# Chunk-selected attention and a phase mixer: query loads of the first groups, an engine for each cast and triangle, token weights by TensorE

## The chip, the cores and the metric

The kernel runs on one core of a Trainium2 chip. The metric is the device time of one execution in microseconds (us). Engines are called PE (TensorE; PEld is its weight load), DVE (VectorE), ACT (ScalarE), POOL (GpSimd) and SP (SyncE, which here only issues DMA transfers). Each engine takes its own instructions strictly in order. Sixteen DMA engines carry the transfers that SP issues.

## The reference

Batch 4, 8 heads, 768 tokens, head size 64; then a mixer over the 512 channels that the heads make together.

```python
k_min, k_max = min and max of k over chunks of 32 tokens          # 24 chunks
ub  = sum_d maximum(q * k_min, q * k_max)                         # per query and chunk
ub  = where(query's chunk >= chunk, ub, -1e9);  top = 6 largest chunks
s   = where(chunk selected and key <= query, q @ k.T / 8, -1e9)
x   = softmax(s) @ v                                              # heads side by side: 768 x 512
theta = x @ w_theta;  zr, zi = x * cos(theta), x * sin(theta)
u   = x + w_tok_r @ zr + w_tok_i @ zi                             # over tokens, 768 x 768 each
out = u + maximum(u @ w_ch, 0)
```

## The kernel before, in words

The work is cut into small tasks. Each is registered by `plan.add` (L36) with the engine that runs it, a duration, what it reads and writes, and a function that emits its instructions. If the engine is given as a table of two, either may run it. The numbers in the table `ORDER` (L153) say in which order all tasks are emitted; a negative entry stands for the task whose number is its complement, on the second engine of its table. `emit` (L62) goes through this list, and so the list alone fixes the order on every engine and in SP's queue. The durations take no part in that.

A *group* (b, g) is half a batch: four heads. For each group:

- `load_kc` (L264) loads the keys of four heads (768 KB, for the first group in two halves), `load_q` (L277) the queries of a pair of heads, 192 KB a head, into a tile `q32` of 128 partitions x 6 blocks x 2 heads x 64, and `load_v` (L286) the values, 96 KB a time. The query view `(n p) d -> p n d` puts token 128n + p on partition p: a partition gets six single rows of 256 B.
- `keys` (L297) takes chunk minima and maxima on DVE (L313, L318, L322) from the fp32 keys. It also casts the keys to fp16 (tile `ke`, L356, POOL), transposes them on PE (L364) and puts them into `kext` (L370, ACT or DVE), the left side of the scores.
- `queries` (L377) transposes the fp32 queries on PE (L399, PSUM tile `psq`), copies them into `ubq` (L405, ACT or DVE) and takes their positive part (L411, POOL or DVE). For the two groups of batch 0 (the set `QPE`, in the code `pe`) `qext`, the right side of the scores, is cast from `ubq` (L417). For all other groups the queries are cast to fp16 into `qe` (L386, POOL), and after the choice a DMA transpose turns `qe` into `qext` (L487).
- `choice` (L422) forms the bounds on PE (L440), adds the causal mask (L448), transposes (L454), finds the six largest by DVE's max of eight (L462) and marks the chunks that are not selected (L476). For batch 0 the marks are transposed on PE (L500, `pss`) and copied into `qext` (L505).
- `values` (L510) casts the values to fp16 on POOL (L514).

`attend` (L523) is one head: scores on PE in three segments (L541, PSUM `psc`), exponentials on ACT (L550, tile `pt`), a triangular mask of 0 and 1 multiplied onto the two diagonal blocks of each segment (`tri`, L561, POOL: 128 x 256 fp16 in place), the product with the values on PE (L575), and the division on DVE (L586, L591) into `x16`. So there are 96 triangles.

`transpose16`, `phases` and `mixer` work on a whole batch: x transposed (L608 by DMA or L619 by PE), theta on PE (L639), sines on ACT (L647), products on DVE (L653), then for each of six blocks of tokens twelve matmuls with `wtokT16` (L681, L683), u (L693), its transpose (L699 by DMA, or L705 by PE and L709), the product with `w_ch` (L717), the last addition (L722) and the store (L726). They run while the next batch attends.

`weights` (L814) loads w_theta and w_ch in four blocks each (`square`, L730: load L733, cast on POOL L734), and the two token matrices in six blocks each (`token`, L737: load L741 of 384 KB, cast on POOL L742). A token block must be transposed. Blocks 2 to 5 (the set `WDMA`) go by a DMA transpose (L746), blocks 0 and 1 by six PE transposes (L754, PSUM `pw`) and a copy into `wtokT16` (L758, ACT or DVE).

At the start 24 `fill` and 12 `rest` tasks run matmuls on zeros (L834, L841) that nothing reads.

Of the kernel before, what the change touches and what calls it, by code (L numbers as in the profile page):

```python
# [75 lines left out]
def kernel(  # L76
# [11 lines left out]
    nc = tc.nc  # L88
    B, H, S, D = q.shape
# [24 lines left out]
    for r in range(96):  # L114
# [39 lines left out]
        17, 0, 15, 3, 14, 8, 2, 4, 1, 5, 13, 82, 6, 113, 114, 115, 70, 83, 19, 85, 20, 21, 63, 22, 23, 64, 24,  # L154
        74, 71, 25, 26, 65, 75, 27, 66, 28, 72, 29, 84, 7, 188, 55, 58, 30, 31, 76, 116, 73, 16, 32, 56, 57, 78,
        90, 86, 33, 91, 69, 34, 289, 92, 77, 67, -94, 290, 87, 9, 35, 79, 36, 89, -89, 37, -95, 80, 126, 117, 81,
        127, 190, 128, 97, 129, 96, 143, 189, 132, 98, 99, 130, 10, 192, 102, 18, 111, 103, 11, 100, 104, 38,
        288, 59, 39, 40, 41, 101, 95, 68, 42, 147, 60, 44, 49, 105, 133, 151, 53, 291, 153, 131, 152, 302, 50,
        46, 62, 134, 54, 301, 304, 135, 154, 118, 106, 120, 303, 305, 107, 191, 61, 139, 193, 306, 108, 174, 121,
        148, 136, 175, 292, 244, 51, 119, 43, 109, 110, -156, 407, 137, 52, 247, 45, 409, 144, 138, 47, 150, 307,  # L160
        -141, 245, 408, 248, 194, 176, 250, 251, 321, 141, 180, 177, 181, 308, -146, -143, 258, 178, 112, -147,
        259, 122, -150, 410, 309, 157, 326, 249, 328, 196, 252, 246, 182, 172, 264, 123, -328, 158, 48, 265, 124,
        156, 329, 179, 325, 293, 261, 310, 262, 296, 183, 125, 184, 185, 272, 195, 275, 420, 12, 163, 159, 273,
        313, 260, 186, 200, 444, 187, 295, 263, 317, 160, 161, 421, 278, 406, 164, 445, 276, 294, 279, 253, 322,
        323, 162, 197, 198, 165, 280, 166, 199, 254, 255, 167, 173, 256, -325, 168, 257, 266, 422, 297, 170, 267,
        286, 311, 423, -172, 312, 201, 344, 298, 299, 204, 269, 268, 616, 345, 169, 300, 358, 277, 274, 346, 618,
        347, 342, 270, 359, 271, -331, -315, -425, 619, 411, 281, 348, 446, 283, 425, 315, 374, 282, 617, 413,
        349, 316, -288, 375, 361, 414, 318, 426, -321, 447, 380, 208, 362, 284, 331, 285, -320, 332, 381, 439,
        343, 205, 360, 364, 350, 365, 336, 333, 351, 372, 334, 377, 373, 388, 337, 335, 352, 615, 415, 412, 382,
        363, 378, 338, 212, 353, 366, 354, 355, 202, 418, 394, 356, 629, 339, 357, 630, -204, 389, 427, 395, 367,  # L170
        631, 632, 340, 206, 369, 379, 416, 391, 376, 435, 209, 215, 417, 392, 431, 368, 210, 370, 371, 207, 211,
        383, 385, 390, 384, 402, 396, 393, 403, 653, 440, 655, 386, 460, 656, 387, 397, 462, -442, 648, 620, 399,
        468, 398, 341, 419, 213, 654, 463, 400, 465, 469, 401, -443, 466, 404, 623, -406, 470, 218, 572, 476,
        732, 464, 467, 216, 214, 575, 436, 480, -438, -439, 622, 443, 461, 221, -658, 477, 478, 217, 481, 471,
        473, 484, 482, 624, 479, 488, 485, 483, 492, 486, 219, 489, 490, 487, 496, 224, 220, 491, 493, 500, 494,
        501, 502, 497, 222, 626, 524, 498, 525, 526, 472, 428, 227, 573, 527, 512, 495, 429, 513, 223, 528, 503,
        504, 514, 499, 576, 733, 627, 625, 578, 586, 529, 474, 430, 225, 574, 579, 634, 505, 600, 226, 230, 587,
        530, 228, 601, 515, 592, 580, 577, 621, 233, 516, 593, 506, 517, 229, 589, 507, 475, 606, 581, 590, 518,
        635, -433, -634, -449, 519, 531, 583, 508, 731, 603, 520, 582, 644, -533, 231, 433, 649, 645, 434, 636,
        536, 584, -652, 594, 647, 537, 236, 650, 538, 734, 640, 604, -647, 539, 591, 234, 540, 607, 541, 449,  # L180
        588, 238, 542, 235, 585, 669, 602, 595, 450, 232, 454, 597, 596, 451, 608, 455, 452, 548, 237, 549, 760,
        598, 453, 550, 736, 240, 551, 456, 239, 552, 605, 457, 242, 599, 735, 764, 560, 553, 458, 609, 745, 746,
        637, 459, 561, 610, 562, 638, 614, 563, 564, 611, 243, 565, 554, 241, 639, 670, 612, 509, 566, 641, 671,
        510, 677, 769, 628, 672, 511, 521, 750, 935, 678, 642, 936, 685, 770, 522, 679, 643, 674, 543, 686, 751,
        737, 523, 658, 652, 613, 934, 688, 673, 752, 675, 544, 739, 700, 663, 689, 676, 937, 533, 659, 938, 753,
        701, 703, 680, 740, 681, 555, 704, 690, 534, 682, 771, 742, 714, 754, 556, 738, 772, 705, 683, 545, 715,
        755, 535, 687, 743, 691, 684, 741, 948, 773, 692, 660, 546, 720, 949, 661, 717, 693, 664, 721, 547, -757,
        718, 694, 702, 706, 707, 765, 696, 665, 722, 695, 662, 767, 708, 697, 666, 972, 667, 747, 719, 766, 698,
        709, 953, 711, 973, 748, 710, 974, 699, 567, 557, 757, 568, 716, 712, -976, 713, 728, 758, 761, 558, 723,
        762, 763, 724, 954, 725, 569, 786, 726, -760, 727, 787, 749, 570, 729, 788, 559, 668, 790, 976, -731,  # L190
        950, 955, 785, 774, 791, 939, 951, 956, 793, 801, 943, 794, 792, 775, 944, 891, 779, 802, 789, 776, 945,
        894, 777, 795, 803, 941, 805, 744, 778, 796, 797, 806, 807, 959, 780, 804, 809, 1050, 942, 1051, 781,
        1052, 798, 813, 810, 782, 811, 940, 571, 808, 817, 814, 812, 821, 783, 815, 818, 825, 816, 819, 826, 822,
        827, 820, 823, 892, 824, 957, 828, 847, 848, 958, 836, 837, 829, 830, 849, 850, 799, 1069, 895, 897, 851,
        831, 960, 838, 800, 898, 896, 893, 905, 919, 839, 832, 906, 852, 1070, 961, 908, 840, 841, 920, 853,
        1071, 907, 899, 900, 901, 902, 768, -1076, 962, 909, 967, 947, 1053, 1064, 842, 911, 990, 833, 912, 903,
        843, 991, 904, 933, 834, 835, 858, 922, 910, 923, 859, 1072, -1066, 784, 996, 860, 921, 861, 925, 913,
        952, 997, 862, 993, 914, 863, 926, 963, 864, 994, 988, 916, 915, 1010, 968, 844, 845, 992, 869, 1004,
        969, 924, 854, 971, 970, 1073, 1055, 917, 870, 1066, 1005, 1067, 1068, 927, 871, 964, 872, -967, 1011,
        873, 1054, 874, 918, 965, 995, 875, 1007, 998, 1008, 1074, 928, 930, 929, 1019, 1020, 1058, 946, 865,  # L200
        876, 1006, 977, 931, 1033, 932, 1056, 846, 999, 1001, 1025, 1021, 978, 1057, 982, 1012, 1018, 1000, 1026,
        1076, 855, 1002, 1034, 1009, 1003, 1083, 856, 983, 979, 1013, 980, 857, 1035, 1027, 1014, 1015, 880, 881,
        1022, 1023, 984, 989, 882, 985, 883, 1036, 981, 1079, 1016, 986, 884, 1017, 885, 1024, 1037, 886, 1039,
        1088, 1040, -1090, 1084, 1038, 1028, -1086, 1059, 887, 1041, 1029, 1030, 1077, 1086, 866, 1031, 1032,
        -1079, 1042, 1090, 867, 1062, 1080, -1092, 1043, -1082, 868, 1047, 1044, -1093, 1082, 877, 1106, 1112,
        1045, 878, 987, 1107, 1093, 1046, 1113, 1048, 1094, 1109, 1114, 1049, 888, 1110, 1098, 1095, 1120, 889,
        1111, 1096, 1108, 1210, 1124, 879, 1121, 1097, 1099, 1115, 1213, 1116, 1122, 1100, 1117, 1125, 1128,
        1123, 1126, 1101, 1132, 1129, 1127, 1130, 1136, 1133, 1131, 1134, 1140, 1137, 1135, 1144, 1138, 1145,
        1141, 1139, 1142, 1146, 1147, 1188, 1189, 1143, 1190, 1191, 1148, 1149, 1150, 1192, 1193, 1194, 1118,
        1211, 1214, 1212, 1216, 1217, 1155, 1063, 1177, 1218, 1178, 1224, 1119, 1225, 1179, 1166, 1230, 1215,  # L210
        1102, 1060, 890, 1167, 1061, 1087, 1151, 1103, 1231, 1232, 1219, 1227, 1228, 1168, 1169, 1180, 1156,
        1220, 1226, 1229, 1181, 1238, 1221, 1239, 1240, 1222, 1223, 1241, 1157, 1242, 1182, 1253, 1233, 1183,
        1158, 1159, 1254, 1259, 1160, 1244, 1170, 1235, 1161, 1234, 1260, 1255, 1162, 1261, 1267, 1171, 1199,
# [15 lines left out]

    UDMA = {(b, t) for b in (1, 2) for t in range(NT)} | {(3, t) for t in range(3)}  # L230
    XDMA = {(b, c) for b in (1, 2, 3) for c in range(3)}
    WDMA = {2, 3, 4, 5}

    QPE = {(0, 0), (0, 1)}
    PSUM = {"sc": 2, "av": 1, "mi": 3}
# [662 lines left out]
```

## Time and profile before

| what | value |
|---|---|
| time, median of 6 runs (lowest to highest) | 256.46 us (254.58 to 256.99) |
| the profiled execution: time, and span in the profile | 256.99 us, 255.2 us |
| PE busy, share of the span | 225.8 us, 88% |
| DVE busy | 173.6 us, 68% |
| ACT busy | 164.5 us, 64% |
| POOL busy | 146.5 us, 57% |
| transfers that SP issues, share of 16 engines | 42.63 MB, 74.5% |
| L561 triangles on POOL | 96, 67.2 us, 0.717 each |
| L356 casts of keys on POOL | 16, 19.2 us, 1.197 each |
| L411 positive part: on POOL / on DVE | 8 at 1.789 / 8 at 0.561 us |
| L386 casts of queries on POOL | 12, 10.8 us, 0.903 each |
| L742 casts of token blocks on POOL | 12, 11.3 us, 0.945 each |
| L746 DMA transposes of token blocks | 8, median 4.8 us from issue to landing |
| L754 PE transposes of token blocks / L758 copies | 24, 2.0 us / 3 on ACT at 0.802, 1 on DVE at 0.545 |

"Busy" is the time in which an engine had an instruction in work; what lies between span and time is outside of the instructions. A stage is read by the engine that has no gap in it, a gap by what ended it. In the chain of waits each step is what released the next one, followed back from the last instruction. An engine that is often idle may still be the one that others wait for, since its queue is in order.

### The profile page before, as it was taken

To read this page: it belongs to the slowest core of one execution; us is meant where nothing else is said; L and a number is where in the kernel's file an instruction comes from. 1 tells how busy PE (TensorE), PEld (TensorE's weight loads), DVE (VectorE), ACT (ScalarE), POOL (GpSimd) and SP (SyncE) were. 2 spreads that over 40 slices of the span, in tenths; PEclk is the share of its full clock that TensorE was granted. 3 is DMA by queue.
4 is the path that set the end of the run, shared out by engine and by line. 5 is a ranking of instruction groups with operands and counts; after the bars stand their busy time and mean duration, and the time that the engine had idled before them with its cause. 6 is when DMAs were issued, how large, how long until landed. Compare 5 with 4: busy or idle time off the path is not lost.

```text
span 255.2 us, 5639 instructions
## 1 busy us (share of the span) xinstructions
PE 225.8 (88%) x2124; PEld 142.8 (56%) x2124; DVE 173.6 (68%) x442; ACT 164.5 (64%) x235; POOL 146.5 (57%) x184
## 2 busy tenths in 40 slices
PE   0976878698799996999789999999999999999993
PEld 0545746567564653568655466667555667644441
DVE  2769875997369789799688875878674134742273
ACT  2384799798689770099469877745987685673001
POOL 6474788969784867669594279994304475300000
PEclk9998879999889999799799999999999999999999
DMA  6999899999999999999987828556901926610334
GB/s 175 259 225 240 164 225 268 237 199 274 199 216 210 216 246 232 193 231 208 219 152 192 192 44 181 110 161 136 156 0 30 181 43 140 178 54 0 82 103 164
DMA packets 99394, 42.98 MB, mean 168 GB/s; under 512 B 92568, under 2 KB 92824, under 8 KB 98696
## 3 DMA queue, kind: packets, MB, share of 16 engines
q1 hardware_dynamic: 99368, 42.63, 74.5%
q8 instruction: 16, 0.26, 0.4%
q14 instruction: 10, 0.08, 0.1%
HBM read 26.30 MB, written 6.29 MB: 128 GB/s over the span
## 4 chain that ended last, share of the span: by engine, by line
PE 54%; DMA 14%; ACT 14%; POOL 7%; DVE 4%; issue 3%; SPq 2%; POOLq 0%; ACTq 0%; DVEq 0%
PE psc L541 9%; ACT pt L550 8%; DMA wtokT<-a 7%; PE psy L681 7%; PE psy L683 7%; PE pso L717 6%; PE pst L639 6%; PE psav L575 5%; DMA qext<-qe 4%; POOL pt L561 3%; PE psub L440 2%; PE psq L399 2%; DMA kc<-in_k_dram 2%; ACT kext L370 2%; PE psz L681 2%
## 5 line engine op out<-in xcount | busy, mean ns | idle before, releaser
L550 ACT ACTIVATE pt<-psc 128x1024 f16<-128x1024 f32 (+1 forms) x96 | 84.7, 917 | 29.3 <-PE psc L541 26.3
L561 POOL TENSOR_TENSOR pt<-pt,tri 128x256 f16<-128x256 f16 x96 | 67.2, 717 | 37.5 <-ACT pt L550 37.2
L541 PE MATMUL psc<-qext,kext 88*128 88x512 f16 (+3 forms) x256 | 53.7, 321 | 6.3 <-ACT pt L550 2.7
L681 PE MATMUL psy<-zz,wtokT 128*128 128x512 f16 x120 | 46.2, 385 | 2.4 <-DMA wtokT<-a 2.4
L541 PEld LDWEIGHTS <-kext 88*128 88x128 f16 x256 | 34.7, 152 | 21.6 <-issue 10.3
L683 PE MATMUL psy<-zz,wtokT 128*128 128x512 f16 x120 | 45.9, 383 | 0.0
L575 PEld LDWEIGHTS <-pt 128*128 128x128 f16 x672 | 29.6, 100 | 8.6 <-DVE x L591 2.2
L575 PE MATMUL psav<-v,pt 128*128 128x65 f16 x672 | 32.4, 197 | 1.4 <-DVE x L591 0.7
L313 DVE TENSOR_TENSOR h<-kc 96x1024 f32<-96x1024 f32 (+1 forms) x16 | 21.9, 1366 | 6.5 <-DMA kc<-in_k_dram 6.4
L717 PE MATMUL pso<-wch,uT 128*128 128x512 f16 x96 | 24.6, 384 | 1.5 <-ACT kext L370 1.0
L681 PEld LDWEIGHTS <-wtokT 128*128 128x128 f16 x144 | 14.2, 99 | 16.6 <-DMA wtokT<-a 2.9
L653 DVE TENSOR_TENSOR zz<-x,cs 128x1024 f16<-128x1024 f16 x24 | 17.3, 727 | 9.1 <-ACT cs L647 8.8
L639 PE MATMUL pst<-wtheta,xT 128*128 128x512 f16 x96 | 23.1, 380 | 0.2 <-ACT cs L647 0.2
L722 DVE SCALAR_TENSOR_TENSOR ot<-pso,u 128x512 f32<-128x512 f32 x24 | 16.5, 687 | 9.5 <-PE pso L717 8.8
L693 DVE TENSOR_TENSOR u<-psy,x 128x512 f16<-128x512 f32 x20 | 13.7, 688 | 13.4 <-PE psy L683 13.2
L405 ACT COPY ubq<-psq 128x384 f32<-128x384 f32 (+1 forms) x26 | 10.9, 425 | 17.9 <-PE psq L399 17.7
L683 PEld LDWEIGHTS <-wtokT 128*128 128x128 f16 x144 | 14.2, 99 | 13.9 <-issue 0.9
L356 POOL CAST ke<-kc 96x1024 f16<-96x1024 f32 x16 | 19.2, 1197 | 3.9 <-DMA kc<-in_k_dram 3.9
L647 ACT ACTIVATE cs<-pst,pi 128x512 f16<-128x512 f32 x24 | 16.6, 692 | 7.1 <-PE pst L639 6.7
L399 PE MATMUL psq<-ident,q 128*128 128x128 f32 x84 | 16.8, 315 | 3.9 <-issue 2.3
L370 ACT COPY kext<-pkt 64x768 f16<-64x768 f16 x16 | 12.7, 794 | 11.0 <-PE pkt L364 8.1
L586 DVE RECIPROCAL rec<-psav 128x6 f32<-128x6 f32 x32 | 6.1, 190 | 18.1 <-PE psav L575 17.8
(76 smaller groups left out, 351.8 us busy)
## 6 DMA issues: line engine op xcount, KB each, us to landing
q<-in_q_dram SPq DMA_DIRECT2D x32, 192.0 KB, 4.3
v<-in_v_dram SPq DMA_DIRECT2D x64, 96.0 KB, 3.5
out_dram<-ot SPq DMA_DIRECT2D x24, 256.0 KB, 2.4
kc<-in_k_dram SPq DMA_DIRECT2D x7, 768.0 KB, 7.2
w<-in_moe_w_tok_r_dram SPq DMA_DIRECT2D x6, 384.0 KB, 4.4
w<-in_moe_w_tok_i_dram SPq DMA_DIRECT2D x6, 384.0 KB, 3.9
w<-in_moe_w_theta_dram SPq DMA_DIRECT2D x4, 256.0 KB, 5.6
w<-in_moe_w_ch_dram SPq DMA_DIRECT2D x4, 256.0 KB, 4.8
```

Source lines behind the costliest of these rows:

```text
L313: nc.vector.tensor_tensor(out=st[hn].rearrange("p (z w) d -> p z (w d)", z=2)[:, s], in0=kv[:, s, 0], in1=kv[:, s, 1], op=op)
L356: nc.gpsimd.tensor_copy(out=ke[:, a:a + 16, :], in_=st[kc][:, a:a + 16, :])
L370: (nc.scalar.copy if e == "ACT" else nc.vector.tensor_copy)(out=kext[g][0:D, a + y:a + 16:2, :], in_=st[pkt][y * D:(y + 1) * D])
L399: nc.tensor.transpose(t[:, o * P:(o + 1) * P], st[q32][:, n, :, :].rearrange("p x d -> p (x d)"), ident32)
L541: nc.tensor.matmul(t[:, a0:a1], kx[0:KX, hj:CH * 96:NCH], qx[0:KX, q0 + a0 - o:q0 + a1 - o], start=True, stop=True)
L550: nc.scalar.activation(out=t[:, BASE[s]:BASE[s] + wa + wb], in_=st[psc][:, 0:wa + wb], func=AF.Exp, bias=0.0, scale=scale)
L561: nc.gpsimd.tensor_tensor(out=d, in0=d, in1=tri16.unsqueeze(1).broadcast_to([P, 2, P]), op=ALU.mult)
L575: nc.tensor.matmul(t[:, a, :], st[pt][:, o:o + P], v16s[g][:, x, j, :], start=(j == 0), stop=(j == a))
L639: nc.tensor.matmul(p, st[xT][:, c, t * P:(t + 1) * P], wtheta16[:, c, :], start=(c == 0), stop=(c == 3))
L681: nc.tensor.matmul(acc(), wtokT16[:, i, 0, t * P:(t + 1) * P], st[zz][:, i, 0, :], start=(i == 0), stop=False)
L683: nc.tensor.matmul(acc(), wtokT16[:, i, 1, t * P:(t + 1) * P], st[zz][:, i, 1, :], start=False, stop=(i == NT - 1))
L717: nc.tensor.matmul(p, st[uT][:, c, :], wch16[:, c, :], start=(c == 0), stop=(c == 3))
```

## The change

1. The queries of groups (0,0) and (0,1) are loaded with `(p n) d -> p n d`: partition p gets the tokens 6p to 6p+5, one run of 1536 B in HBM. The tile is the same. PE's transposes then give the columns in another order (block n holds the tokens 6p + n), and the copies L405 of these groups put each column at its place, with a step of six elements on the side they write.
2. The casts of keys, queries, token blocks and square weights, and the triangles, may each go to POOL or DVE.
3. `WDMA` is empty: all twelve token blocks are transposed by PE and copied by ACT or DVE. This makes eight tasks more (1414 for 1406), and all task numbers after them move.
4. `ORDER` is another list throughout. Some of the durations beside the tasks are other numbers, which has no effect of its own.

What the two lists say, counted by engine:

| task | before | after |
|---|---|---|
| triangles (L561) | POOL 96 | POOL 64, DVE 32 (batches 0 to 3: 12, 5, 4, 11 on DVE) |
| casts of keys (L356) | POOL 16 | POOL 13, DVE 3 |
| casts of queries (L386) | POOL 12 | POOL 6, DVE 6 |
| casts of token blocks (L742) | POOL 12 | POOL 8, DVE 4 |
| casts of square weights (L734) | POOL 8 | POOL 7, DVE 1 |
| positive part (L411) | POOL 8, DVE 8 | POOL 2, DVE 14 |
| copies into kext (L370) | ACT 16, DVE 16 | ACT 22, DVE 10 |
| copies of token blocks (L758) | ACT 3, DVE 1 | ACT 9, DVE 3 |
| copies of queries (L405) | ACT 26, DVE 6 | ACT 24, DVE 8 |
| tasks on PE, ACT, DVE, POOL, SP | 522, 227, 279, 178, 200 | 530, 236, 330, 126, 192 |

In SP's queue the eight query loads of batch 0 stand at places 2, 5, 7, 8, 10, 11, 16, 22 before and 2, 5, 6, 8, 9, 11, 12, 14 after; the halves of the first keys at 1 and 6, then 1 and 4; the keys of (0,1) at 9, then 15; the first values at 14, then 18; the causal mask at 12, then 16.

```diff
-    WDMA = {2, 3, 4, 5}
+    WDMA = set()
...
+    def eng(e):
+        return nc.gpsimd if e == "POOL" else nc.vector
...
-                nc.sync.dma_start(out=t[:, :, x, :], in_=q[b, 2 * p + x].rearrange("(n p) d -> p n d", p=P))
+                nc.sync.dma_start(out=t[:, :, x, :], in_=q[b, 2 * p + x].rearrange(
+                    "(p n) d -> p n d" if (b, p // 2) in QPE else "(n p) d -> p n d", p=P))
...
-                nc.gpsimd.tensor_copy(out=ke[:, a:a + 16, :], in_=st[kc][:, a:a + 16, :])
-            plan.add("POOL", 1.1, key, cast, r=rk[0] if a == 0 else rk[-1] if parts == 2 else rk[0], w=[("ke", a)])
+                eng(e).tensor_copy(out=ke[:, a:a + 16, :], in_=st[kc][:, a:a + 16, :])
+            plan.add({"POOL": 1.1, "DVE": 0.68}, None, key, cast, lock=True, r=rk[0] if a == 0 else rk[-1] if parts == 2 else rk[0], w=[("ke", a)])
...
-                nc.gpsimd.tensor_copy(out=qe[:, x0:x0 + 2, :, 0:D], in_=st[q32].rearrange("p n x d -> p x n d"))
+                eng(e).tensor_copy(out=qe[:, x0:x0 + 2, :, 0:D], in_=st[q32].rearrange("p n x d -> p x n d"))
...
-                (nc.scalar.copy if e == "ACT" else nc.vector.tensor_copy)(
-                    out=st[ub][:, QN + t0 + off:QN + t0 + w], in_=st[psq][:, off:w])
+                o, i_ = st[ub][:, QN + t0 + off:QN + t0 + w], st[psq][:, off:w]
+                if pe:
+                    o = st[ub][:, QN:].rearrange("d (p n) -> d n p", n=NT)[:, t0 // P:(t0 + w) // P]
+                    i_ = i_.rearrange("d (n p) -> d n p", p=P)
+                (nc.scalar.copy if e == "ACT" else nc.vector.tensor_copy)(out=o, in_=i_)
...
-                nc.gpsimd.tensor_tensor(out=d, in0=d, in1=tri16.unsqueeze(1).broadcast_to([P, 2, P]),
+                eng(e).tensor_tensor(out=d, in0=d, in1=tri16.unsqueeze(1).broadcast_to([P, 2, P]),
                                         op=ALU.mult)
-            plan.add("POOL", 0.66, key, tri, r=["tri"], w=[(pt, s)])
+            plan.add({"POOL": 0.66, "DVE": 0.28}, None, key, tri, r=["tri"], w=[(pt, s)], lock=True)
...
-        plan.add("POOL", 0.84, key, lambda: nc.gpsimd.tensor_copy(out=new(a), in_=st[n]), r=[n], w=[(a, 0)],
-                 new=[(a, "a16")])
+        plan.add({"POOL": 0.84, "DVE": 0.55}, None, key, lambda e: eng(e).tensor_copy(out=new(a), in_=st[n]), r=[n], w=[(a, 0)],
+                 new=[(a, "a16")], lock=True)
```

The cast of the square weights (L734) is changed in the same way as the last of these.

## The prediction

> **What bounds the kernel now.** I read the busy time in 40 slices first, then stages of it, then the chain of waits where PE (TensorE) stands still. The first view (one digit per 6.4 us, 9 is full):
>
> ```profile
> PE   0976878698799996999789999999999999999993
> ...
> ACT  2384799798689770099469877745987685673001
> ...
> PEclk9998879999889999799799999999999999999999
> DMA  6999899999999999999987828556901926610334
> ```
>
> To see: the 16 DMA engines are full for the first twenty slices (to about 128 us), and from there PE is full to the end. PE's gaps, and the slices in which its clock was granted at 0.7 or 0.8, lie in the part where DMA is full. The same by stage (columns: stretch, length, busy us of PE, PEld, DVE, ACT, POOL with their counts, clock, DMA share, GB/s):
>
> ```profile
> 29.00:59.30 30.30, 25.07 (x334) 19.57 (x334) 25.07 (x80) 27.70 (x39) 24.79 (x33) 0.94 0.93 229
> ...
> 68.20:95.20 27.00, 26.74 (x232) 15.68 (x228) 20.90 (x33) 22.84 (x32) 18.33 (x21) 0.94 1.08 224
> 95.20:108.80 13.60, 11.18 (x95) 6.35 (x85) 11.55 (x36) 0.35 (x3) 9.93 (x14) 0.87 1.10 213
> 108.80:130.70 21.90, 19.35 (x225) 14.45 (x224) 18.01 (x51) 16.56 (x25) 15.39 (x20) 0.92 0.99 216
> 130.70:255.20 124.50, 119.28 (x1014) 69.18 (x1010) 73.75 (x185) 76.44 (x102) 52.69 (x69) 1.00 0.50 113
> ```
>
> From 29 to 59 us ACT is the tightest (27.70 of 30.3) with DVE behind it. From 95 to 109 ACT does 0.35 us of work. From 130.7 on PE is busy 119.3 of 124.5 us, 3.7 of the rest being the end of the span. PE is busy 225.8 of the 255.2 us in all, so 29.4 us are idle: 6.6 before its first instruction, the tail, and some 18 between 7 and 131 us. Only these can be won.
>
> Two places explain most of them. PE around the first scores (start, length, line):
>
> ```profile
> 20.34 0.59 PE L841 MATMUL fill<-zero 128*128 128x122 f16 x8
> 23.23 0.52 PE L399 MATMUL psq<-ident,q 128*128 128x128 f32 x3 [2.30 <-issue]
> ...
> 26.53 0.74 PE L500 MATMUL pss<-ident,a 128*128 128x128 f16 x5
> 28.04 0.59 PE L541 MATMUL psc<-qext,kext 88*128 88x512 f16 x3 [0.77 <-ACT qext L505]
> ```
>
> The choice of group (0,0) leaves DVE at 21.76 us, but its transposes (L500) run at 26.5: PE takes its queue in order, and ahead of them stand the query transposes (L399) of pairs 2 and 3, whose loads were issued between 11.7 and 24 us. And the chain around 95 us:
>
> ```profile
> 88.71 5.06 DMA wtokT<-a
> 93.92 0.83 POOL a L742
> 95.16 1.51 SPq L746
> 96.72 4.87 DMA wtokT<-a
> 101.64 0.39 PE psy L681
> ```
>
> Token weights come through a load, a GpSimd cast and a DMA transpose of about 5 us; mixer(0) waits for the last at 101.6. Query transposes behind it in PE's queue wait too, so ACT stands still.
>
> **The change, part by part.** Prices come from the groups by shape, of which two (count, busy us, mean ns of one, idle before):
>
> ```profile
> L653 DVE TENSOR_TENSOR zz<-x,cs 128x1024 f16<-128x1024 f16 x24 | 17.3, 727 | 9.1 <-ACT cs L647 8.8
> ...
> L619 PE MATMUL psT<-ident,x 128*128 128x128 f16 x42 | 3.8, 232 | 0.0
> ```
>
> (1) *Loads reordered.* In SP's queue the eight query loads of groups (0,0) and (0,1) move from places 2, 5, 7, 8, 10, 11, 16, 22 to 2, 5, 6, 8, 9, 11, 12, 14, past the keys of (0,1) (place 9 to 15) and the first values. The fourteen loads up to the last query hold 2.7 MB (keys 0.79, queries 1.57, the rest constants and one weight block); at the 232 GB/s that the stretch 5 to 29 us shows that is 11.7 us, and with 3 us to the first bytes all queries are in by about 15, and L399 no longer stands ahead of L500. The second half of the first keys goes from place 6 to 4, some 1 us earlier of its 8.8. What is late instead: keys (0,1), the mask and the values, by two us, or by five if (2) gives nothing; keys (0,1) feed a transpose ahead of L500, so L500 falls to about 21.5, not to the choice's end. Gain: 26.5 - 21.5 = **5.0 us**. Bounds: 2 (queue order alone, keys late) and 6.5 (choice also 1.5 earlier).
>
> (2) *Six rows to a run.* The loads read 1536 B per partition instead of 256 B. A price isn't in the trace; between nothing and the difference of a 192 KB load at the 168 GB/s mean (1.17 us) and at 281 GB/s, the fastest early stretch (0.70): 0 to 0.47 each, 0 to 3.8 in all. It is inside (1); I take none of it on its own, because the tile keeps 256 B pieces on the SBUF side.
>
> (3) *Strided evictions.* The eight L405 copies of these groups now write with a step of six floats. L405 takes 0.48 contiguous; the farthest strided row, L322, takes 1.04 us for 512 elements against 0.68 for L318 undisturbed, a factor of 1.5. So 0 to 0.26 each; two or three lie on the first chain, up to 0.8, inside the lower bound of (1). The Trainium skill (SBUF — State Buffer, Door 1: The DMA port swizzle) says that steps past a 16-byte line cost extra, which speaks against this edit; it gives no figure for the engine, so by it the sum would only move to that bound.
>
> (4) *Triangles and casts to DVE.* In all 32 triangles, 14 casts and 6 more relus go from GpSimd to DVE. Before the choice of (1,0) the stage 29 to 59 us takes, by the order: 8 triangles, 3 casts, a few other moves, less 3 evictions of L370. A DVE triangle isn't in the trace: by L653 per element 0.18 us, by L591 (384 elements, 0.553) 0.37; I take 0.28 between, so 2.2. A cast by L411 per element (0.446 median for 576) 0.6 to 0.8, by L313 (1024 in 1.46) up to 1.5; I take 0.6 to 0.8 as the same kind of one-input pass: 2.0. The others sum to -0.9. DVE's 25.1 become 28.4 of 30.3 us, 94%, on an engine that takes its queue in order; ACT's work there is unchanged within 0.5. It loses **1.5 us** (0 if it all fits the idle 5.2; 3.7 with its dear ends). Up to the choice of (2,0) the order puts 17 triangles (4.8), 10 casts (6.5), two relus (0.9) and two evictions of token weights (1.1) more on DVE and six L370 evictions (0.55 each, 3.3) less: 10.0 us; GpSimd sheds some 28 (18 triangles at 0.72, 10 casts at 0.95, three relus at 1.79).
>
> The row for DVE and GpSimd together: one L411 shape on DVE goes from 440 to 873 ns. The Trainium skill (same page, Who interferes with whom) says that casts and two-input operations of VectorE take a port pair that GpSimd needs, and one blocks the other; by it each moved cast also stops GpSimd, and the sum would lose a further 2 us in this stage (an estimate, three casts at 0.7). GpSimd falls from 24.8 to about 16 us of these 30, so I leave that out.
>
> (5) *Token weights by TensorE.* Eight DMA transposes go. One of 131 KB alone (208 to 209 us) held the engines 0.63 of 1 us, so 196 KB take 0.95, 7.6 in all, and their eight issues of 1.25 leave SP's queue. The last weight then follows its load: before, the last load was issued at 88.1 and the last transpose landed at 101.6. Between 68.2 and 130.7 PE is idle 0.26 + 2.42 + 2.55 = 5.2 us, and its clock (0.87 and 0.92 in the last two stretches: 0.13 of 11.2 and 0.08 of 19.4 us) costs 3.0 us more. I take 3.0 of the idle and 1.5 of the clock: **4.5 us** (0 to 8.2). Against it, 48 PE transposes: L619 3.8/42 = 0.09 each, 4.3, of which 0.8 fall into what idle is left: **3.5 us** lost. The eight evictions (six on ACT at 0.80, two on DVE at 0.55) are hidden by ACT's idle 13.2 us of 95 to 109; if that cover goes, ACT's 4.8 count.
>
> (6) From 131 us PE is full and its work is the same: 0. DVE has 50 us of slack there for the other 15 triangles.
>
> Sum: -5.0 + 1.5 - 4.5 + 3.5 = **-4.5 us**. The profiled execution took 256.99 with a span of 255.2, so 252.5; the median is 256.46, 0.5 lower, so **252.0**.
>
> **Rivals.** *VectorE becomes the bound.* DVE is busy 99.9 of the first 130.7 us, 5 of the rest lie before the first keys, and ten more leave little; each late choice delays the queries' transposes and the scores. For: 94% in the stage above, in-order queue. Against: DVE's contention falls with GpSimd's work. It decides once more than 4.5 + 1.5 of these ten come out ahead of something awaited; at nine, 252.0 - 1.5 + 9 = 259.5. *PE was the bound all along.* The gaps only move into the next stage, ACT and DVE hold the early gain back, and the 4.3 us of new transposes eat the rest: 256. *All of it lands.* -6.5 - 8.2 + 3.5 = -11.2, with DVE's 1.5 hidden: 245.3, and in parts up to 250. *The loads do not get faster* because SBUF's side keeps 256 B: queries end 3 us later, (1) gives 3.5: 253.5.
>
> **Chances.** Forecast (250 to 254.5) 0.45; loads no faster (253.5) 0.08; everything lands 0.12; PE-bound, no change 0.14; VectorE bound 0.21. About 0.5% (1.3 us) can be told from nothing here. Faster 0.45 + 0.08 + 0.12 = 0.65, same 0.14, slower 0.21. The range takes the forecast, both neighbours and half of each outer case: 246.5 to 260; the forecast's own is 250 to 254.5.
>
> **What would show it.** L500 before 23 us and the first exponential (L550) before 25.5 show (1). Fewer small packets show (2). L405 at 0.48 or 0.7 decides (3). DVE over 95% between 25 and 60 us shows the first rival. PE's first mixer product no longer waiting on wtokT, and ACT busy between 90 and 105, show (5). I am wrong if the first scores are early but those of batch 2 start later than 126 us (130.7 before).

## The result and the profile after

The changed kernel takes 255.88 us (median of 37 runs, 251.95 to 261.17) beside 257.19 us (79 runs, 254.58 to 263.06) for the kernel before on the same chips. The ratio is **0.9898, 95% interval 0.9874 to 0.9921**: 1.0% or **2.6 us** faster (0.0102 of 257.19). A ratio leaves out the executions that are over 1.5% above the fastest of their kernel (21 of the 37 here, and the profiled ones of e8 and e11, which are not read), and medians leave out none. The medians are only 1.3 us apart, so the size of the gain is known to a factor of two, and the table of experiments gives both. The two profiled executions, 252.52 us after (span 250.7) and 256.99 before (span 255.2), differ by 4.5 us: the look at the changed kernel happens to be one of its quicker executions.

The slices of the span after:

```profile
PE   8775987798799999997999999999998999999983
...
ACT  2479898999799877873898667485984277491000
...
PEclk9999599999999999999999999999999999999999
DMA  6997999989898999999751467696131637600333
```

The DMA engines are full up to slice 19 (119 us) instead of 20, the hole that ACT had in slices 16 and 17 is gone, and PE's clock is lowered in one slice, not in seven (mean granted clock 0.986 beside 0.967; other executions of the kernel before reach 0.992, so part of this can belong to the execution). By stage, in the stretches that the prediction used (columns as there):

```profile
29.00:59.30 30.30, 25.33 (x332) 19.63 (x331) 28.24 (x92) 28.80 (x46) 18.91 (x24) 0.95 0.96 244
68.20:95.20 27.00, 26.75 (x254) 16.45 (x255) 25.86 (x64) 23.89 (x34) 13.71 (x18) 1.00 0.98 239
95.20:108.80 13.60, 13.60 (x158) 9.46 (x157) 12.65 (x33) 11.16 (x16) 9.41 (x14) 1.00 1.26 240
108.80:130.70 21.90, 19.83 (x186) 12.63 (x185) 17.42 (x41) 15.43 (x26) 9.03 (x12) 1.00 0.78 188
130.70:250.70 120.00, 113.56 (x973) 65.65 (x971) 71.83 (x196) 67.42 (x91) 30.93 (x43) 1.00 0.44 102
```

The third line is the change: from 95 to 109 us ACT goes from 0.35 to 11.16 us of work and PE from 11.18 to 13.60, with no gap at all. In the first line DVE has risen from 25.07 to 28.24 of 30.3 us. In the last PE is idle 6.4 us.

Where the chain before had a load, a cast and a DMA transpose one after the other, the chain of waits after holds PE alone:

```profile
91.83 0.34 PE pkt L370 x8
92.17 0.34 PE pw L763 x6
92.70 0.22 PE psy L690
...
99.71 0.31 PE psc L550 x2
```

The token transposes (L763) stand between mixer products (L690) and scores (L550), and nothing is waited for.

### The profile page after: what moved, and what is told of

Same layout as the page of the kernel before. It is cut to its first block, busy times and chain, and to the rows that moved or that the text cites. A ratio compares the mean times of both kernels' runs of the same rounds, so it can differ in the third digit from the quotient of the medians.

```text
span 250.7 us, 5746 instructions
## 1 busy us (share of the span) xinstructions
PE 226.2 (90%) x2172; PEld 142.0 (57%) x2172; DVE 183.9 (73%) x493; ACT 172.3 (69%) x244; POOL 98.9 (39%) x132
## 2 busy tenths in 40 slices
DMA packets 92995, 41.42 MB, mean 165 GB/s; under 512 B 86168, under 2 KB 86424, under 8 KB 92296
## 4 chain that ended last, share of the span: by engine, by line
PE 62%; ACT 12%; DMA 12%; DVE 7%; SPq 5%; issue 1%; DVEq 0%; ACTq 0%
PE psc L550 10%; PE psy L690 10%; PE psy L692 9%; PE pst L648 7%; PE pso L726 7%; ACT pt L559 6%; PE psav L584 6%; DMA uT<-u 3%; DMA kc<-in_k_dram 3%; DMA qext<-qe 3%; PE psub L449 2%; SPq L288 2%; PE psz L692 2%; PE psz L690 2%; DMA kext<-onehot 2%; ACT kext L376 2%
## 5 line engine op out<-in xcount | busy, mean ns | idle before, releaser
L559 ACT ACTIVATE pt<-psc 128x1024 f16<-128x1024 f32 (+1 forms) x96 | 86.0, 921 | 32.3 <-PE psc L550 30.5
L570 POOL TENSOR_TENSOR pt<-pt,tri 128x256 f16<-128x256 f16 x64 | 44.9, 712 | 76.8 <-ACT pt L559 59.5
L550 PE MATMUL psc<-qext,kext 88*128 88x512 f16 (+3 forms) x256 | 53.0, 322 | 5.4 <-ACT pt L559 1.9
L690 PE MATMUL psy<-zz,wtokT 128*128 128x512 f16 x120 | 45.5, 379 | 0.7 <-ACT uT L718 0.7
L550 PEld LDWEIGHTS <-kext 88*128 88x128 f16 x256 | 34.1, 153 | 20.3 <-issue 7.9
L584 PEld LDWEIGHTS <-pt 128*128 128x128 f16 x672 | 28.3, 98 | 6.9 <-issue 0.5
L584 PE MATMUL psav<-v,pt 128*128 128x65 f16 x672 | 31.1, 194 | 0.2 <-POOL a L751 0.2
L690 PEld LDWEIGHTS <-wtokT 128*128 128x128 f16 x144 | 14.1, 98 | 13.1
L319 DVE TENSOR_TENSOR h<-kc 96x1024 f32<-96x1024 f32 (+1 forms) x16 | 18.4, 1151 | 3.8 <-DMA kc<-in_k_dram 3.8
L415 ACT COPY ubq<-psq 128x384 f32<-128x384 f32 (+1 forms) x24 | 12.6, 524 | 10.3 <-PE psq L405 10.3
L600 DVE TENSOR_TENSOR x<-psav,rec 128x384 f16<-128x384 f32 x32 | 17.7, 553 | 0.7
L376 ACT COPY kext<-pkt 64x768 f16<-64x768 f16 x22 | 17.4, 794 | 1.1 <-PE pkt L370 0.8
L523 POOL CAST v<-v 128x768 f16<-128x768 f32 x16 | 13.5, 851 | 11.7 <-DMA v<-in_v_dram 11.4
L405 PE MATMUL psq<-ident,q 128*128 128x128 f32 x84 | 15.4, 293 | 2.9 <-issue 1.2
```

What stands on the lines that cost most here:

```text
L319: nc.vector.tensor_tensor(out=st[hn].rearrange("p (z w) d -> p z (w d)", z=2)[:, s], in0=kv[:, s, 0], in1=kv[:, s, 1], op=op)
L376: (nc.scalar.copy if e == "ACT" else nc.vector.tensor_copy)(out=kext[g][0:D, a + y:a + 16:2, :], in_=st[pkt][y * D:(y + 1) * D])
L550: nc.tensor.matmul(t[:, a0:a1], kx[0:KX, hj:CH * 96:NCH], qx[0:KX, q0 + a0 - o:q0 + a1 - o], start=True, stop=True)
L559: nc.scalar.activation(out=t[:, BASE[s]:BASE[s] + wa + wb], in_=st[psc][:, 0:wa + wb], func=AF.Exp, bias=0.0, scale=scale)
L570: eng(e).tensor_tensor(out=d, in0=d, in1=tri16.unsqueeze(1).broadcast_to([P, 2, P]), op=ALU.mult)
L584: nc.tensor.matmul(t[:, a, :], st[pt][:, o:o + P], v16s[g][:, x, j, :], start=(j == 0), stop=(j == a))
```

## Where the time went

A mark that all runs share is the choice of the second group of batch 1: its bounds on PE (`psub`), and then its two DMA transposes into `qext`, without which the last heads of batch 1 have no scores. `psub` in the timeline of PE before:

```profile
94.18 1.31 PE L440 MATMUL psub<-ubq,bnd 64*32 64x320 f32 x32
```

and after:

```profile
83.97 1.31 PE L449 MATMUL psub<-ubq,bnd 64*32 64x320 f32 x32
```

It comes 10.2 us earlier. In the old list all products of four of the six token blocks of mixer(0) stand ahead of it in PE's queue (blocks 0, 2, 1, 3); in the new one those of two (0 and 1). The switch of ACT from exponentials to the sines of batch 1 then comes 10.25 us earlier as well (123.95 for 134.20). So the old gap of ACT from 95 to 109 us was a group of scores whose choice came late. Three things stood in front of these scores. The bounds stood behind four mixer blocks in PE's queue. The choice left DVE at 99.43, and its two transposes were issued only at 102.09, behind the last two token transposes and four loads in SP's queue (after: 90.68 and 91.50):

```profile
95.16 3.88 SPq L746 DMA_TRANSPOSE wtokT<-a  x2
...
102.09 5.57 SPq L487 DMA_TRANSPOSE qext<-qe  x2
```

And the first scores themselves (108.07) stood behind the products of blocks 4 and 5, which waited for `wtokT` until 101.64. How much each of the three is worth is not shown: they overlap in time.

By the end 4.5 us of the 10.25 are left. From ACT's switch to the end PE does 115.8 us of work before (965 matmuls) and 120.3 after (1011): some 4.5 us of PE's work now stands behind the mark instead of ahead of it, and PE idles 1.2 us more. The lead was partly a change of order and not of length.

## The experiments

Each ran beside the kernel before. For each the table gives the ratio, the ratio of the medians of all executions, the span of its profiled execution, the time at which the transposes of that choice are issued, and what follows it.

| kernel | ratio to before (95%) | of medians | span, us | choice issued, us | rest, us |
|---|---|---|---|---|---|
| before | 1 | 1 | 255.2 | 102.1 | 153.1 |
| after | 0.9898 (0.9874 to 0.9921) | 0.995 | 250.7 | 91.5 | 159.2 |
| e1_rows | 0.9872 (0.9823 to 0.9920) | 0.988 | 253.0 | 94.4 | 158.6 |
| e2_onehot | 0.9811 (0.9723 to 0.9899) | 0.996 | 249.2 | 90.4 | 158.8 |
| e3_wdma | 1.0229 (1.0175 to 1.0282) | 1.024 | 260.2 | 102.4 | 157.8 |
| e4_tripool | 1.0023 (0.9989 to 1.0058) | 1.001 | 255.6 | 95.6 | 160.0 |
| e5_casts | 0.9845 (0.9787 to 0.9904) | 0.987 | 253.6 | 94.4 | 159.2 |
| e6_tokonly | 1.0132 (1.0077 to 1.0188) | 1.019 | 259.8 | 109.1 | 150.7 |
| e7_trionly | 1.0041 (0.9986 to 1.0095) | 1.012 | 257.3 | 103.8 | 153.5 |
| e8_both | 0.9799 (0.9733 to 0.9865) | 0.996 | | | |
| e9_toktri | 1.0141 (1.0064 to 1.0218) | 1.017 | 258.8 | 108.4 | 150.4 |
| e10_start | 1.0058 (1.0014 to 1.0103) | 1.006 | 257.9 | 105.0 | 152.9 |
| e11_best | 0.9826 (0.9741 to 0.9911) | 0.989 | | | |
| e12_toktri32 | 1.0216 (1.0165 to 1.0267) | 1.022 | 262.7 | 109.2 | 153.6 |

The last column shows two families: with the new list 157.8 to 160.0 us follow the choice, with the old one 150.4 to 153.6. Within a family a kernel is as late as this choice is, within 2 to 3 us. That is one profiled execution of each kernel, and a mark that goes with the end need not be its cause: e6, e9 and e12 have it within 0.8 us of each other and end up to 3.9 us apart. The new list gains 10.6 us before the mark and gives back 6.1 after it.

### e1_rows: the query layout undone

```diff
-  "(p n) d -> p n d" if (b, p // 2) in QPE else "(n p) d -> p n d", p=P))
+  "(n p) d -> p n d", p=P))
...
-  if pe:
-      o = st[ub][:, QN:].rearrange("d (p n) -> d n p", n=NT)[:, t0 // P:(t0 + w) // P]
-      i_ = i_.rearrange("d (n p) -> d n p", p=P)
```

> The changed kernel with one part undone: queries of batch 0 loaded as before (token 128n + p on partition p) and their copies out of PSUM written without a step; the order of all tasks stays. Theory A (the six-row runs bring nothing: the changed kernel has 6,399 packets fewer, which is eight token transposes at 800, so its query loads still go in 256 B pieces; and each strided copy costs 0.35 us): packets stay at about 93,000, the ACT copies of batch 0 fall from 0.83 to 0.48 us, the first scores come 0 to 0.6 us earlier than 25.3, and the time is the changed kernel's or up to 1 us less, ratio to before 0.986 to 0.990. Rival B (the runs do speed the loads): the last queries come 2 to 4 us later, the first scores after 27, ratio 0.995 to 1.00.

The ratio, 0.9872, cannot be told from that of the changed kernel. The transfers of the changed kernel in the profile:

```profile
DMA packets 92995, 41.42 MB, mean 165 GB/s; under 512 B 86168, under 2 KB 86424, under 8 KB 92296
```

and those with the old layout:

```profile
DMA packets 92995, 41.42 MB, mean 164 GB/s; under 512 B 86168, under 2 KB 86424, under 8 KB 92296
```

The same packets, to the last one: a run of 1536 B in HBM is still cut into the 256 B pieces of the tile. What the layout costs is seen in the copies out of PSUM (count, then shortest, median and longest in ns), after:

```profile
L415 ACT COPY ubq<-psq x24: 307/476/875, 8.6 to 185.6; 128x384 f32<-128x384 f32 x16, 128x192 f32<-128x192 f32 x8
```

A copy of 384 columns with a step of six floats takes up to 0.875 us beside 0.476 without. In the time the part saves nothing that can be told, and it costs a little on ACT and DVE. The loads may land a little earlier with it, though: the causal mask stands behind the queries in SP's queue, and it lands 9.0 us after its issue in e1 and 7.4 to 8.4 us in the five profiles that have the new layout and are read (after, e2 to e5). The first scores of e1 come at 26.90, those of the five at 24.72 to 26.17. This is the direction of rival B, and short of its size.

### e2_onehot: the one-hot load earlier

In the changed kernel PE's first score matmul waits for the one-hot rows:

```profile
25.27 1.06 PE L550 MATMUL psc<-qext,kext 88*128 88x512 f16 x3 [1.80 <-DMA kext<-onehot]
```

The edit moves one number of `ORDER`:

```diff
+        11,
         55,
...
-        11,
```

> The changed kernel with one load moved in SP's queue: the first one-hot block (144 KB) from place 26 to place 18, ahead of the first values. In the changed kernel's profile the first scores at 25.27 wait 1.8 us for it. Theory A (the start is carried to the end): first scores at 24.1, time 1.0 to 1.3 us less than the changed kernel's, ratio to before 0.985. Rival B (the stage up to 60 us is held by VectorE and ScalarE, which are 93% busy there, and takes the gain back): first scores at 24.1, first scores of batch 1 at 65.4 as before, ratio 0.990.

The wait is gone (first scores at 24.72 us, then held 0.55 us by ACT's copy into `qext`). The ratio is 0.9811, but it rests on two executions (251.04 and 253.90 us), its interval overlaps that of the changed kernel, and the median of all six is no better (0.996 beside 0.995). Whether the earlier load shortens the kernel is open.

### e3_wdma: token blocks 2 to 5 by DMA again, in the new list

```diff
-    WDMA = set()
+    WDMA = {2, 3, 4, 5}
```

> The changed kernel with one part undone: token blocks 2 to 5 go by DMA transposes again, issued at the places where the PE transposes stood; the eight copies out of PSUM are gone. Theory A (part 5 is the larger half of the gain): the engines' DMA share stays near 1 to 115 us or longer, ScalarE falls idle between 85 and 105 us, and the time is 2.5 to 5 us more than the changed kernel's, ratio 1.00 to 1.01. Rival B (token weights were hidden and PE only got 4 us more work): 2 to 4 us less than the changed kernel's, ratio 0.975 to 0.982.

1.0229: against the changed kernel 3.3%, **8.5 us** (1.0229 - 0.9898 = 0.0331, of 257 us), where the prediction had 1.0 net and theory A 2.5 to 5. The profile shows two prices that neither had. A cast on DVE (timeline of DVE, e3; in brackets what it waited for):

```profile
84.54 0.56 DVE L752 CAST a<-w 128x768 f16<-128x768 f32 x1 [3.74 <-DMA wtokT<-a]
```

The cast needs a free fp16 buffer, and that is held until the DMA transpose has read it. Before, GpSimd had these waits (5.8 us in all). The new list has three of the casts for these blocks on DVE, where all later work stands behind them. PE waits in turn:

```profile
86.82 1.30 PE L450 MATMUL psub<-ubq,bnd 64*32 64x320 f32 x30 [2.44 <-DVE u L703]
```

The larger price is in SP's queue. The choice leaves DVE at 95.31 (90.68 in the changed kernel), and its first transpose is issued 7.1 us later (there 0.8), behind loads and two of the token transposes:

```profile
96.82 1.57 SPq L756 DMA_TRANSPOSE wtokT<-a  x1
...
99.06 1.22 SPq L756 DMA_TRANSPOSE wtokT<-a  x1
...
102.38 1.44 SPq L497 DMA_TRANSPOSE qext<-qe  x1
```

So of the 10.9 us by which the mark of the table is later, 4.6 lie before the end of the choice and 6.3 in SP's queue.

### e4_tripool: all triangles back on GpSimd, in the new list

```diff
-    ... -255, -180, ... -258, ... -261, ...
+    ... 254, 179, ... 257, ... 260, ...
```

(32 entries of `ORDER`: each negative entry is a triangle on DVE, its complement the same task on POOL)

> The changed kernel with all 96 triangles on GpSimd again; nothing else moves. VectorE loses 10.2 us of work, GpSimd gains 23. Theory A (VectorE's triangles are worth little either way; neither engine is the bound after 60 us): within 1 us of the changed kernel, ratio 0.986 to 0.994. Rival B (VectorE, 93% busy from 23 to 53 us, is what holds that stage): first scores of batch 1 come 1 to 2 us earlier and the ratio is 0.982 to 0.986. Rival C (the order counts on the short VectorE triangles): products with the values wait for GpSimd, ratio 0.996 to 1.01.

1.0023: by the ratios the triangles on DVE are worth 1.25%, **3.2 us**, in this list; by the medians about half of that. The profile of e4 shows a way in which they can be, on DVE:

```profile
32.93 4.11 DVE L421 TENSOR_SCALAR ubq<-ubq 128x576 f32<-128x576 f32 x1 [0.86 <-ACT ubq L416]
```

and on GpSimd:

```profile
32.99 3.18 POOL L571 TENSOR_TENSOR pt<-pt,tri 128x256 f16<-128x256 f16 x5
36.12 0.61 POOL L744 CAST wtheta<-w 128x512 f16<-128x512 f32 x1
37.16 1.53 POOL L571 TENSOR_TENSOR pt<-pt,tri 128x256 f16<-128x256 f16 x1 [0.44 <-ACT pt L560]
```

A VectorE instruction that takes 0.46 us (its median) lasts 4.11: as long as GpSimd runs triangles and a cast without a gap. It ends at 37.04, in GpSimd's first pause. A key-tree step at 53.23 lasts 3.07 beside its usual 1.2. Together that is 5.5 us on DVE. PE stands 2.00 us behind the first of them:

```profile
38.93 0.36 PE L585 MATMUL psav<-v,pt 128*128 128x65 f16 x6 [2.00 <-DVE x L601]
```

By 74 us this execution is 4.5 us behind that of the changed kernel (ACT's first switch at 74.51, not 70.03). How much of this the long instructions make is not shown: the execution of e5 is 3.3 us behind at the same place (73.30), and e5 is not slower. The ratio lies in the range of rival C, but not for its reason: PE waits only 0.7 us for GpSimd's triangles.

### e5_casts: the fourteen casts back on GpSimd, in the new list

```diff
-    ... -83, ... -310, ... -198, ...
+    ... 82, ... 309, ... 197, ...
```

(14 entries of `ORDER`: three casts of keys, six of queries, four of token blocks and one of a square block)

> The changed kernel with the 14 casts (3 of keys, 6 of queries, 4 of token blocks, 1 of a square weight) on GpSimd again, same order. In the changed kernel's profile they take VectorE 9.7 us; on GpSimd at its rows 12.6 us. Theory A (what counts is how long a cast holds back the next in the chain, as with the triangles): 1 to 3 us more than the changed kernel, ratio to before 0.993 to 1.00. Rival B (GpSimd, 39% busy, takes them for nothing, and VectorE gains room): the changed kernel's time or up to 1 us less, ratio 0.985 to 0.991.

0.9845 (0.9787 to 0.9904): moving the casts to DVE brings nothing; without it the kernel may be slightly faster.

### e6_tokonly and e9_toktri: token weights by TensorE in the old list

e6 has the old list with blocks 2, 4 and 5 by PE; block 3 stays with DMA.

```diff
-    WDMA = {2, 3, 4, 5}
+    WDMA = {3}
```

> The kernel before with the token weights alone changed, and of these six of the eight blocks (2, 4 and 5 of both matrices): PE transposes and a copy near the place of the DMA transpose; block 3 stays with the DMA, since no place in the old order has a PSUM buffer free for it. All else is the kernel before. Theory A (the gain of part 5 is there by itself): ScalarE's gap between 95 and 109 us shrinks to under 7 us, 2 to 5 us less than before, ratio 0.980 to 0.993. Rival B (in the old order something else ends the wait, and PE gets 3 us more work): ratio 0.995 to 1.01.

1.0132: the same part that is worth 8.5 us in the new list costs 3.4 us in the old one, with six of its eight blocks. At the place of interest, DVE in e6:

```profile
91.18 6.31 DVE L413 TENSOR_SCALAR ubq<-ubq 128x576 f32<-128x576 f32 x2
97.42 0.41 DVE L711 COPY uT<-psut 128x512 f16<-128x512 f16 x1
```

GpSimd:

```profile
91.73 1.26 POOL L358 CAST ke<-kc 96x1024 f16<-96x1024 f32 x1
92.94 0.82 POOL L744 CAST a<-w 128x768 f16<-128x768 f32 x1
93.73 1.29 POOL L563 TENSOR_TENSOR pt<-pt,tri 128x256 f16<-128x256 f16 x2
94.97 0.82 POOL L744 CAST a<-w 128x768 f16<-128x768 f32 x1
95.75 0.66 POOL L563 TENSOR_TENSOR pt<-pt,tri 128x256 f16<-128x256 f16 x1
96.36 0.82 POOL L516 CAST v<-v 128x768 f16<-128x768 f32 x1
```

and PE:

```profile
97.88 0.84 PE L366 MATMUL pkt<-perm,ke 96*128 96x96 f16 x13 [3.49 <-DVE uT L711]
```

PE's wait for the DMA transposes is gone, and what was held by them is now ready at once: GpSimd gets its casts and triangles back to back, one of the two positive parts on DVE (0.45 us elsewhere) takes 5.47 us, and PE waits 3.49 us for the copy behind it. The choice is issued at 109.1, seven us later than before. The wait is half of that, and a slower PE behind it is some more: the granted clock is 0.50 from 98.7 to 101.5 us, where mixer products come 0.43 us apart instead of 0.21. Before, the same follows the wait of 2.41 us at 101.64 (0.50 from 103.3 to 105.9).

e9 was to add the 32 triangles on DVE to e6. Its expectation speaks of these; by a slip in numbering the kernel that ran moved one triangle only, so it is e6 once more.

> The kernel before with two parts at once and its old order: the token blocks 2, 4 and 5 by TensorE (as in e6, 1.0132 alone) and the 32 triangles on VectorE (as in e7, 1.0041 alone). In e6's profile one VectorE relu of 0.45 us took 5.47 us while GpSimd ran triangles and casts without a gap from 91 to 98 us, and TensorE stood 3.49 us behind it. Theory A (the parts hang together: GpSimd's back-to-back work holds VectorE up, and the triangles taken off GpSimd lift that): the two together are better than the sum of both alone, 0.985 to 1.000, and no VectorE instruction is over 3 us. Rival B (the gain is in the changed order, the parts in the old order only cost): 1.013 to 1.022, about the sum of both.

1.0141, and the long instruction again (6.31 us for the pair at 90.44): the stall belongs to the order of the work and not to chance.

### e7_trionly and e12_toktri32: triangles on DVE in the old list

```diff
-  plan.add("POOL", 0.66, key, tri, r=["tri"], w=[(pt, s)])
+  plan.add({"POOL": 0.66, "DVE": 0.28}, None, key, tri, r=["tri"], w=[(pt, s)], lock=True)
```

with the same 32 triangles on DVE as in the changed kernel; e7 has this alone, e12 on top of e6.

> The kernel before with the triangles alone changed: the same 32 as in the changed kernel go to VectorE, in the old order. Theory A (a triangle of 0.3 instead of 0.7 us shortens the way from the exponentials to the product with the values wherever it stands): 1.5 to 3.5 us less than before, ratio 0.986 to 0.994. Rival B (the gain seen when they are undone belongs to the new order alone; VectorE is 83% busy here from 29 to 59 us and its queue holds other work): ratio 0.996 to 1.01.

> What e9 was meant to be: in e9 a numbering slip moved one triangle to VectorE instead of 32, so it was e6 once more (1.0141 beside 1.0132, and the same 5 us long relu at 91 us). Here the kernel before, in its old order, has the token blocks 2, 4 and 5 by TensorE and all 32 triangles of the changed kernel on VectorE. Theory A (the parts hang together: GpSimd's back-to-back work holds VectorE up, and fewer triangles there lift that): 0.985 to 1.000, and no VectorE instruction over 3 us. Rival B (the gain is in the changed order; in the old order the parts only cost): 1.010 to 1.022. A long relu gone and a ratio over 1.01 together would mean that the stall is real but not what decides.

e7: 1.0041, no gain. e12: 1.0216, slower than either part alone. My theory that the two parts help each other whatever the order has fallen. The long instruction is still there (5.69 us for the pair at 91.86), because only one of the triangles around it is among those that moved. So the parts pay only in the list that was written with them, and the list needs the parts: e3 and e4 take one away and lose 8.5 and 3.2 us.

### e10_start: the new sequence of first loads in the old list

```diff
-        0, 3, 8, 2, 4, 1, 5, 6, 113, 114, 115, 7, 188, 55, 58, 116, ...
+        0, 3, 2, 1, 4, 5, 8, 114, 6, 9, 116, 115, 188, 117, 113, 7, 10, 55, 58, ...
```

(task numbers of SP alone, in its queue's order)

> The kernel before with one edit: its first 24 loads stand in the changed kernel's sequence (second key half fourth, the queries before the second group's keys, cmask and tri before the first values). All else as before. Theory A (the first term of the forecast's sum, a gain of 5.0 us by the start): 0.980, first score matmul before 25.5 us, span some 5 us under 255.2. Rival B (the start of the one profile before was a late one: e6 and e7 have the same start and put the first pss matmul at 23.05 and 23.45 us, not 26.53, and the first scores at 25.3 and 25.1): 0.995 to 1.005.

1.0058 (1.0014 to 1.0103): no gain, rather 1.5 us of loss. The edit did more than move queries, though. `perm`, the matrix with which PE transposes keys, goes from place 3 to 7 in SP's queue, and in the old list a key transpose is PE's first task:

```profile
8.76 0.80 PE L365 MATMUL pkt<-perm,ke 96*128 96x96 f16 x8 [8.76 <-DMA perm<-perm]
```

Before, it starts at 6.61, the first bounds are at 16.53 and the first scores at 28.04; in e10 these are at 18.92 and 27.33. So e10 alone cannot say what earlier queries are worth. That there was little to win is seen in other profiles. PE around the first choice before:

```profile
23.23 0.52 PE L399 MATMUL psq<-ident,q 128*128 128x128 f32 x3 [2.30 <-issue]
```

and in e7, which has the same loads in the same order:

```profile
21.18 0.52 PE L401 MATMUL psq<-ident,q 128*128 128x128 f32 x3
23.45 0.44 PE L502 MATMUL pss<-ident,a 128*128 128x128 f16 x5
25.11 0.66 PE L543 MATMUL psc<-qext,kext 88*128 88x512 f16 x3 [1.23 <-DMA kext<-onehot]
```

The wait of 2.30 us "for nothing that the profile shows" belonged to one execution. In e6, e7, e9 and e12, all with the old start, `pss` begins at 23.05, 23.45, 24.11 and 22.86 and the scores at 25.1 to 25.5; the changed kernel has 22.80 and 25.27. Beside these there was next to nothing to win.

### e8_both and e11_best: candidates

e8 is the changed kernel with e1's layout and e2's load; e11 adds e5's casts on GpSimd.

> The changed kernel with the query loads and copies as before (part 2 undone) and the first one-hot block ahead of the first values. Theory A (the two gains add, since the copies are shorter and the wait for the one-hot block is gone): first scores at 24.5 or earlier, ratio 0.977 to 0.983. Rival B (without the reordered rows the queries come later, and the early start is lost): first scores at 26 or later as in the run with the rows undone, ratio 0.984 to 0.990.

> The changed kernel with three parts altered: the one-hot load ahead of the first values (e2, 0.9811 to before), the query layout of before (e1, 0.9872) and the 14 casts back on GpSimd (e5, 0.9845). Theory A (each of these is worth a little by itself and they add up): 0.970 to 0.980 to before. Rival B (they are all the changed kernel within the scatter of runs, 0.9898): 0.985 to 0.992.

0.9799 and 0.9826. By these ratios both are some 2% faster than the kernel before, and the interval of e8 ends just before that of the changed kernel begins (0.9865 and 0.9874). But each ratio rests on three executions (251.41 to 254.11 us for e8, of twelve; 251.30 to 255.04 for e11, of six), and both were picked out of several candidates. The medians of all executions are 0.996 and 0.989 of the kernel before, where the changed kernel has 0.995. Neither is shown to be better than the change itself.

## Why the prediction was right, and where its steps were not

The forecast was 252.0 us, a gain of 4.5, with 250 to 254.5 as its own range; measured were 2.6 us of gain by the ratio and 1.3 by the medians. As a time, the median of 255.88 lies above its own range and inside the whole one, 246.5 to 260. The sign was right. But the runs show that the sum came out near the truth by luck: large errors cancelled.

- **Term (1), -5.0 us, failed.** It took the 26.53 us of the first `pss` as a property of the load order and read "[2.30 <-issue]" as query transposes waiting for their loads. It was one execution's wait: four other executions of that start have 22.9 to 24.1 (e10 cannot price the new loads, because of `perm`). The mask, which the term named as late, was given no price: at place 16 it holds the first choice, for which DVE waits 1.33 us in the changed kernel and not at all before. `pss` before 23 came true (22.80), exponentials before 25.5 did not (26.36), and the first could have come true without any edit.
- **Term (2), 0**: right, and its reason too; e1 has the same packets. Its sign, fewer small packets, would have misled: there are 6,399 fewer than before (92995 for 99394), but they belong to the eight token transposes, for e3, which has these again beside the new layout, has 99395.
- **Term (3), 0 to 0.26 us each, was too small.** The row taken for strided access gave a factor of 1.5; measured is 1.8 on ACT (0.875 to 0.476). The Trainium skill (SBUF — State Buffer, Door 1: The DMA port swizzle), cited there for the cost of steps past a 16-byte line, agrees in direction; it gives no size for this.
- **Term (4), +1.5 us, had the load right and the sign wrong for the triangles.** DVE was forecast at 28.4 of 30.3 us, and is 28.24. A DVE triangle takes 0.328 us (forecast 0.28), a key cast 0.682 and a query cast 0.698 (0.6 to 0.8). But in the new list triangles on DVE bring 3.2 us (e4) and the casts nothing (e5). What the term left out is what GpSimd's work does to DVE, not DVE's to GpSimd: with GpSimd down from 146.5 to 98.9 us, the large step of the key tree falls from 1.464 to 1.218 us and the next from 0.990 to 0.763, and DVE's total rises by only 10.3 us. With the triangles back (e4, GpSimd 120.1 us) the large step takes 1.365, but the next one 0.709, so only the first goes with GpSimd's work.
- **Term (5), -4.5 + 3.5 = -1.0 us, was mis-sized**: taken away in the new list, the part costs 8.5 us. The price of the transposes was right (forecast 4.3 us, measured 6.0 - 2.0 = 4.0). What was too small is the gain: the term knew PE's idle and clock in two stretches, but not that the group of scores queued behind the mixer could come forward. It counted the eight issues that leave SP's queue, but not what they hold back there: the transposes of a choice (in e3 these stand 6.3 us longer in the queue). Its signs both came true (ACT busy from 95 to 109, no wait for `wtokT`). In the old list six of the eight blocks cost 3.4 us, so the gain belongs to part and list together.
- **Term (6), 0 after 131 us, failed.** The lead at ACT's second switch is 10.25 us and 4.5 at the end. I had asked only whether the work after 131 us was the same, not whether work would be moved there.
- **No term for the list.** Parts alone in the old list: first loads +1.5 (with the late `perm`), triangles +1.0, tokens +3.4, tokens and triangles +5.6 us; all together with the new list -2.6. So the list, with the parts that it was made for, is worth some 8 us, and the prediction priced it at the start only. Which of its moves does it is not shown by a run: that the choice of group (1,1) stands behind two mixer blocks and not four is read from the list and fits the rows of the table but one: in e3 the bounds are nearly as early as in the changed kernel (86.82 and 83.97), and the rest of the delay is SP's queue. Moving the choice alone wasn't tried, nor was the new list without any of the parts.
- **Rivals.** VectorE did not become the bound: 28.24 of 30.3 us, and PE never waits on it for more than 1.2 us at a time. "PE was the bound all along" (256) is nearest to the median of all executions, 255.88, and half of its mechanism came: of the lead of 10.25 us, 5.75 are given back where PE is full. But the gap from 95 to 109 us was closed and not moved, and the first exponentials of batch 2 come at 119.96 (130.74 before), well under the 126 that would have shown the forecast wrong. "The loads do not get faster" was right in that the packets stay the same.

## What to carry to other kernels

A gap in one profile is worth a gain only if other executions have it: a wait put down to "issue" should be looked up in a second look before it is priced. When a change brings a new order along, ask what that order moves ahead of the old gap, since parts and order can be worth 8 us together and the parts lose alone. Look at the queue that issues transfers as at any other engine: what stands in it ahead of an awaited transfer counts. And an engine that becomes less busy can be a gain for its neighbour, even where nobody waits for it. When one constant is loaded later, ask which engine needs it first.

## What the runs showed of the hardware

VectorE can be held up by GpSimd for several instructions on end. A positive part of 128 x 576 floats, 0.45 us alone, took 4.11 us (e4), 5.47 (e6) and 4.85 (e12) while GpSimd ran triangles and casts without a pause; before, the longest was 0.87, but a key-tree step of 1.2 us took 2.98 (at 99.81). The Trainium skill (SBUF — State Buffer, Who interferes with whom) has the two engines share a port pair that one of them holds for a whole instruction while the other waits. These rows agree, and go further: the wait is not over with one GpSimd instruction of 0.6 to 1.3 us, but lasted through six in e4 and seven in e6. In e4 it ended in GpSimd's first pause; in e6 GpSimd had none, and the triangle that it then ran took 0.87 us for 0.66. The other way round is seen too: triangles on GpSimd take 0.66 us at best and up to 1.64.
